# Moving the squares and RMS scales of query blocks 2 to 4 ahead of the loads in an attention + SwiGLU kernel

## The chip, the cores and the metric

The kernel runs on one core of a Trainium2 chip. The metric is device time in microseconds (us) of one execution; two executions of the kernel before were timed. The engines are named as the profile names them: PE (matrix multiply; PEld is its weight load), ACT (activations), DVE (vector), POOL (a second, general vector engine, which here also issues most loads) and SP (a queue that issues the other loads and all stores).

## The reference, cut to what matters

```python
# B=8 batches, H=8 heads, S=576 positions, D=64
scores = 0.125 * q @ k.T                       # per batch and head
scores = where(causal, -1e9, scores + minimum(-(cum_i - cum_j), 0))   # cum = cumsum(max(s, 0))
attn   = softmax(scores) @ v
x      = attn, heads side by side              # 4608 tokens x 512
rms    = sqrt(mean(x*x) + 1e-6)                # per token
xn     = x / rms * rms_g
out    = (silu(xn @ w_gate) * (xn @ w_val)) @ w_out      # 512 -> 1536 -> 512
```

## The kernel before

The work goes in turns. `attention(b)` makes one batch: 8 units (a pair of heads, `hp`, by a half of the query positions, `hf`), each with its scores on PE, `Exp` on ACT into `E` (L277), a causal mask on POOL (the affine selects, L279 and L283), the product with the values on PE (AV, L301) and a division on DVE into `x_blk` (L305, L306). `x_blk` has five blocks of 128 tokens. A block then takes three steps to reach `xnT`, the transposed and normalised input of the FFN:

- `att_square(a, tb)`: ACT squares block `tb` and sums each row (L313).
- `att_alpha(a, t0, t1)`: POOL turns the sums of several blocks into 1/rms, the tile `al` (L318, then a power, L320).
- `att_scale(a, tb)`: DVE multiplies the block by `al` (L323). `att_out(a, tb)`: four transposes on PE into `psX` (L330), then DVE writes `xnT` (L334).

Blocks 0 and 1 are complete after the fifth unit and take these steps inside `attention`. Blocks 2 to 4 are complete only after the last unit; they are this case's subject.

The FFN is cut into 9 chunks of 512 tokens. `ffn1(c)` has 12 groups: 16 matmuls of 256 columns or 8 of 512 into a pair of PSUM banks `psD` (L345, two pairs in turn), then `Silu` on ACT (L351) and a product on DVE into `H_sb` (L352). Here group n is called g0 to g11. Between groups `ffn1` runs fillers, each with a position between 0 and 1: a filler at p stands behind the first group for which (i + 1) / 12 >= p. The second half, `ffn2_steps` (L373, with the copy L378), is dealt out inside the next `attention`. So chunk c follows attention of batch c, and its first groups run before blocks 2 to 4 of that batch are in `xnT`. Everything is in program order: each engine takes its instructions in the order in which the program lists them, and waits for the one in front.

The fillers of chunk c hold, besides the three blocks: `load_kq(c + 2)` and `load_v(c + 2)` at 0.1 (five loads each of k and q on POOL, five of v on SP), `prep_v(c + 1)` on POOL (L237, five, from 0.2) with `prep_w` (L248), and the transposes of k and q of batch c + 1 (L211; for batch 1 L201, with DVE packs L191) from 0.4, or 0.66 in chunk 0. Ahead of chunk 0 stand, on POOL, the loads of k and q of batch 1 (L111), of `w_out` (L124) and of v (L118).

Of the kernel before, what the change touches and what calls it, by code (L numbers as in the profile page):

```python
# [10 lines left out]
def kernel(  # L11
# [83 lines left out]
    def ps_x():  # L95
        return pp.tile([128, CC, 128], bf16, name="psX", tag="AT", bufs=2)
# [156 lines left out]
    def att_begin(b):  # L253
        a = Att()
        a.b = b
        a.x = mp.tile([128, NB, DM], bf16, name="x_blk", tag="x_blk", bufs=2)
        a.ss = mp.tile([128, NB], fp32, name="ss", tag="ss", bufs=2)
        a.al = mp.tile([128, 2, NB], fp32, name="al", tag="al", bufs=2)
        a.E = {}
        return a  # L260

    def unit_scores(a, u):
        hp, hf = u % HP, u // HP
        st = ps_pair()
        if hf == 0:
            groups = ((0, 0, 0, 256), (1, 256, 128, 384))
        else:
            groups = ((2, 0, 256, 512), (3, 256, 384, 576), (4, 448, 512, 576))
        for i, (kb, c0, q0, q1) in enumerate(groups):
            for j in range(2):  # L270
                rs = slice(j * 64, j * 64 + 64)
                nc.tensor.matmul(  # L272
                    st[:, j, c0 : c0 + q1 - q0], lhsT=KT[rs, hp, kb * 128 : kb * 128 + 128],
                    rhs=QT[rs, hp, q0:q1],
                    start=(i == 0), stop=(i == len(groups) - 1))
        E = a.E[u] = mp.tile([128, 2, DM], bf16, name="E", tag="E", bufs=7)
        nc.scalar.activation(out=E, in_=st, func=AF.Exp, scale=0.125)  # L277
        diag = E.rearrange("p j (c n) -> p (j c) n", n=128)[:, 0:8:2, :]
        nc.gpsimd.affine_select(out=diag, in_=diag, pattern=[[0, 4], [1, 128]],  # L279
                                compare_op=ALU.is_ge, fill=0.0, base=0, channel_multiplier=-1)  # L280
        if hf == 1:
            last = E[:, :, 448:512]
            nc.gpsimd.affine_select(out=last, in_=last, pattern=[[0, 2], [1, 64]],  # L283
                                    compare_op=ALU.is_ge, fill=0.0, base=0,
                                    channel_multiplier=-1)
# [26 lines left out]
    def att_square(a, tb):  # L312
        nc.scalar.activation(out=sq_scr[:, 0:DM], in_=a.x[:, tb, :], func=AF.Square,  # L313
                             accum_out=a.ss[:, tb : tb + 1])

    def att_alpha(a, t0, t1):
        m, y = a.al[:, 0, t0:t1], a.al[:, 1, t0:t1]
        nc.gpsimd.tensor_scalar(out=m, in0=a.ss[:, t0:t1], scalar1=1.0 / DM, scalar2=1e-6,  # L318
                                op0=ALU.mult, op1=ALU.add)
        nc.gpsimd.tensor_tensor(out=y, in0=m, in1=mhalf[:, 0 : t1 - t0], op=ALU.pow)  # L320

    def att_scale(a, tb):
        nc.vector.tensor_scalar(out=a.x[:, tb, :], in0=a.x[:, tb, :],  # L323
                                scalar1=a.al[:, 1, tb : tb + 1], scalar2=None, op0=ALU.mult)

    def att_out(a, tb):
        p0 = 64 if tb == 4 else 0
        X = ps_x()
        for cc in range(CC):
            nc.tensor.matmul(X[:, cc, :], lhsT=a.x[:, tb, cc * 128 : (cc + 1) * 128],  # L330
                             rhs=ident_bf, is_transpose=True,
                             start=(cc == 0), stop=(cc == CC - 1))
        c0 = a.b * S + tb * 128
        nc.vector.tensor_tensor(  # L334
            out=xnT[:, :, c0 : c0 + 128 - p0], in0=X[:, :, p0:128],
            in1=g_sb.unsqueeze(2).to_broadcast([128, CC, 128 - p0]), op=ALU.mult)
# [46 lines left out]
    def spread(fns, lo, hi):  # L383
        n = len(fns)
        return [(lo + (hi - lo) * i / n, f) for i, f in enumerate(fns)]
# [9 lines left out]
        f.append((0.8, lambda: prep_w(b, nc.gpsimd)))  # L395
        return f

    def tail_fillers(a, lo, hi):
        fns = [lambda tb=tb: att_square(a, tb) for tb in (2, 3, 4)]
        fns += [lambda: att_alpha(a, 2, 5)]  # L400
        fns += [lambda tb=tb: (att_scale(a, tb), att_out(a, tb)) for tb in (2, 3, 4)]
        return spread(fns, lo, hi)

    def take(filler, n):
        for _ in range(n):
            next(filler, None)

    def attention(b, filler, lead, each):
        a = att_begin(b)
        take(filler, lead[0])  # L410
        unit_scores(a, 0)
        take(filler, lead[1])
        unit_scores(a, 1)
        take(filler, lead[2])
        for u in range(2 * HP):
            if u + 2 < 2 * HP:
                unit_scores(a, u + 2)
            unit_av(a, u)
            if u == HP:
                for tb in (0, 1):  # L420
                    att_square(a, tb)
                att_alpha(a, 0, 2)
            if u == HP + 2:
                for tb in (0, 1):
                    att_scale(a, tb)
                if not each:
                    for tb in (0, 1):
                        att_out(a, tb)
            if b and u < HP:
                prep_peak(b, u)  # L430
            take(filler, each)
        if each:
            for tb in (0, 1):
                att_out(a, tb)
            for _ in filler:
                pass
        return a

    whole = [(0, DM, fb) for fb in range(FB)]
# [4 lines left out]
    with tc.manual_schedule():  # L444
        nc.sync.dma_start(out=s_all, in_=s.rearrange("b h s -> (b h) s"))
        nc.sync.dma_start(out=g_sb, in_=moe_rms_g.rearrange("(cc p) -> p cc", p=128))
        load_runs(0, 0, 0, 4)
        load_runs(0, 1, 0, 4)
        make_identity(nc, ident_bf)
        load_runs(0, 0, 4, 8)  # L450
        load_runs(0, 1, 4, 8)
        make_identity(nc, ident_F)
        load_v(0, nc.gpsimd)
        for i in range(2):
            load_w(0, i * FH, (i + 1) * FH)
            load_w(1, i * FH, (i + 1) * FH)
        nc.vector.memset(ones, 1.0)
        nc.vector.memset(w_row[:, S : NB * 128], 0.0)
        nc.vector.memset(KT[:, :, S : NB * 128], 0.0)
        nc.vector.memset(vw[64:128, 4, :, :], 0.0)  # L460
        nc.vector.memset(mhalf, -0.5)
        nc.vector.memset(k_nat[64:128, :, 4, :, :], 0.0)
        nc.vector.memset(nrm, 0.0)
        nc.vector.memset(hones, 0.0)
        nc.vector.memset(hones[0:64, 0:1], 1.0)
        nc.vector.memset(hones[64:128, 1:2], 1.0)
        decay_a()
        for g in range(2):
            prep_pack(0, 4 * g, 4 * g + 4)
            prep_pack(1, 4 * g, 4 * g + 4)  # L470
            if g == 0:
                decay_b()
            for hp in (2 * g, 2 * g + 1):
                prep_transpose(0, 0, hp)
                prep_transpose(0, 1, hp)
        prep_w(0, nc.scalar)
        for sc in range(NB):
            prep_v(0, sc, nc.vector)
        a = attention(0, iter(()), (0, 0, 0), 0)
        load_runs(1, 0)  # L480
        load_runs(1, 1)
        load_w(2, 0, 6)
        load_w(2, 6, 12)
        load_v(1, nc.gpsimd)
        for c in range(NCH):
            fillers = []
            if c < B:
                fillers += tail_fillers(a, 0.0, 0.25 if c == 0 else 0.4)
            if c == 0:
                fillers += spread([lambda hp=hp: prep_peak(0, hp) for hp in range(HP)], 0.3, 0.6)  # L490
                fillers += spread([lambda i=i: prep_norm(0, i) for i in range(3)], 0.3, 0.6)
                fillers += prep_fillers(1, 0.66, 1.0)
            elif c + 1 < B:
                fillers += prep_fillers(c + 1, 0.4, 0.98)
            if c + 2 < B:
                for w in range(2):
                    fillers.append((0.1, lambda b=c + 2, w=w: load_kq(b, w)))
                fillers.append((0.1, lambda b=c + 2: load_v(b, nc.sync)))
            if c == B:
                check_decay()  # L500
                check_all()
            Ht = ffn1(c, quarters if c == 0 else halves if c < 4 else whole, fillers)
            fl = ffn2_steps(c, Ht)
            if c + 1 < B:
                a = attention(c + 1, fl, (8, 4, 6), 3)
            else:
                for _ in fl:
                    pass
# [166 lines left out]
```

## Time and profile before

| | |
|---|---|
| median of two executions | 505.26 us (503.77 and 506.76) |
| the profiled execution | 506.42 us, of which the trace's span is 504.7 |
| PE busy | 395.9 us (78% of the span) |
| DVE, ACT, POOL busy | 230.7, 215.1, 172.3 us |
| mean granted TensorE clock | 0.925 of full |

The busy time of a row counts an engine's instructions, with matmul ends modelled. Times in rows are us from the span's start. A wait is put down to what came last before the waiting instruction. PEclk is the granted TensorE clock as a share of 2.4 GHz, so 0.50 is 1.2 GHz.

### The profile page before, as it was taken

The numbers are of one execution on the slowest core, as the hardware profiler recorded it, in microseconds if no ns is written. First come the engines' busy times: TensorE is split into PE (matmuls) and PEld (weight loads), VectorE is DVE, ScalarE is ACT, GpSimd is POOL, SyncE is SP. The second block draws the span as 40 slices with busy tenths as digits, with TensorE's granted clock in tenths as the row PEclk, the third lists the DMA queues.
The fourth block names the chain that finished last, engine by engine and source line by source line (L and its number), as shares of the span: only waits on it lengthen the run. The fifth ranks groups of instructions, "written<-read, shape, count | busy, mean of one in ns | idle before, by whom it ended". The sixth has DMA issues, their size and how long they took to land.

```text
span 504.7 us, 7722 instructions
## 1 busy us (share of the span) xinstructions
PE 395.9 (78%) x3083; PEld 226.9 (45%) x3083; DVE 230.7 (46%) x461; ACT 215.1 (43%) x351; POOL 172.3 (34%) x267
## 2 busy tenths in 40 slices
PE   3740068697799779986998699959995999697995
PEld 2530047545584558455844254425442544243442
DVE  6730035565336634563355435643564356433331
ACT  2830006583257425751565156615652566120220
POOL 8651540049204930393039403940224022000000
PEclk9985559999899989998999899989998999998898
DMA  9999950019701980199019901990110011002002
GB/s 151 199 197 195 183 26 0 2 43 153 78 0 43 144 88 2 43 129 101 1 43 121 109 0 44 113 117 1 38 46 1 0 44 44 0 1 83 1 2 88
DMA packets 97803, 33.75 MB, mean 67 GB/s; under 512 B 85856, under 2 KB 92512, under 8 KB 97760
## 3 DMA queue, kind: packets, MB, share of 16 engines
q0 software_dynamic: 63840, 16.52, 34.5%
q1 hardware_dynamic: 33920, 16.67, 14.0%
q8 instruction: 26, 0.43, 0.3%
q14 instruction: 17, 0.14, 0.1%
HBM read 37.90 MB, written 9.44 MB: 94 GB/s over the span
## 4 chain that ended last, share of the span: by engine, by line
PE 57%; DMA 12%; POOL 10%; DVE 9%; ACT 8%; issue 4%; SPq 0%; ACTq 0%; POOLq 0%
PE psD L345 35%; PE psO L373 11%; DMA v_nat<-in_v_dram 8%; PE psT L211 4%; PE psX L330 3%; DMA xnT<-in_k_dram 3%; DVE H_sb L352 3%; ACT S_sb L351 3%; DVE x_blk L323 2%; POOL al L320 2%; POOL q_nat L105 2%; PE psAV L301 2%; ACT E L277 2%; POOL E L279 2%; PE psD L272 2%
## 5 line engine op out<-in xcount | busy, mean ns | idle before, releaser
L351 ACT ACTIVATE S_sb<-psD 128x512 bf16<-128x512 f32 x108 | 64.3, 595 | 240.1 <-PE psD L345 239.7
L352 DVE TENSOR_TENSOR H_sb<-S_sb,psD 128x512 bf16<-128x512 bf16 x108 | 74.2, 687 | 165.1 <-ACT S_sb L351 165.1
L345 PE MATMUL psD<-xnT,wg_sb 128*128 128x256 bf16 (+1 forms) x624 | 121.9, 335 | 0.0
L345 PE MATMUL psD<-xnT,wv_sb 128*128 128x256 bf16 (+1 forms) x624 | 118.3, 327 | 0.0
L279 POOL TENSOR_SCALAR_AFFINE_SELECT E<-E 128x512 bf16<-128x512 bf16 x64 | 41.1, 642 | 213.1 <-ACT E L277 212.9
L373 PE MATMUL psO<-wout_sb,H_sb 128*128 128x512 bf16 x432 | 107.4, 379 | 0.0
L345 PEld LDWEIGHTS <-wv_sb 128*128 128x128 bf16 x624 | 64.1, 103 | 38.0 <-issue 5.3
L330 PE MATMUL psX<-ident_bf,x_blk 128*128 128x128 bf16 x160 | 17.4, 238 | 77.6 <-DVE x_blk L323 77.5
L345 PEld LDWEIGHTS <-wg_sb 128*128 128x128 bf16 x624 | 60.1, 104 | 30.9 <-issue 2.8
L277 ACT ACTIVATE E<-psD 128x1024 bf16<-128x1024 f32 x64 | 63.6, 1023 | 8.0 <-PE psD L272 7.7
L373 PEld LDWEIGHTS <-H_sb 128*128 128x128 bf16 x432 | 36.9, 98 | 34.9 <-issue 3.0
L330 PEld LDWEIGHTS <-x_blk 128*128 128x128 bf16 x160 | 10.6, 104 | 90.6 <-DVE x_blk L323 87.6
L378 DVE COPY osb<-psO 128x512 f32<-128x512 f32 x36 | 24.8, 688 | 29.1 <-PE psO L373 29.1
L301 PE MATMUL psAV<-vw,E 128*128 128x65 bf16 x576 | 32.3, 199 | 6.2 <-POOL E L279 4.3
L237 POOL TENSOR_TENSOR vw<-v_nat,wT 128x512 bf16<-128x512 f32 (+1 forms) x35 | 35.5, 1044 | 0.0
L301 PEld LDWEIGHTS <-E 128*128 128x128 bf16 x576 | 23.6, 100 | 20.1 <-POOL E L279 10.7
L323 DVE TENSOR_SCALAR x_blk<-x_blk,al 128x512 bf16<-128x512 bf16 x40 | 18.9, 489 | 29.8 <-POOL al L320 29.3
L306 DVE TENSOR_TENSOR x_blk<-psAV,rZ 128x256 bf16<-128x256 f32 (+1 forms) x64 | 31.4, 491 | 2.2
L334 DVE TENSOR_TENSOR xnT<-psX,g_sb 128x512 bf16<-128x512 bf16 (+1 forms) x40 | 24.8, 636 | 14.3 <-PE psX L330 13.7
L105 POOL DMA_DIRECT2D k_nat<-in_k_dram x30 | 25.8, 880 | 12.2 <-DMA wout_sb<-in_moe_w_out_dram 7.7
L272 PE MATMUL psD<-QT,KT 64*128 64x256 bf16 (+2 forms) x320 | 26.7, 266 | 0.9 <-ACT E L277 0.9
L105 POOL DMA_DIRECT2D q_nat<-in_q_dram x30 | 25.4, 901 | 1.6 <-DMA v_nat<-in_v_dram 1.6
(80 smaller groups left out, 289.9 us busy)
## 6 DMA issues: line engine op xcount, KB each, us to landing
out_dram<-osb SPq DMA_DIRECT2D x36, 256.0 KB, 2.0
v_nat<-in_v_dram SPq DMA_DIRECT2D x24, 256.0 KB, 9.7
k_nat<-in_k_dram POOLq DMA_DIRECT2D x24, 128.0 KB, 4.5
q_nat<-in_q_dram POOLq DMA_DIRECT2D x24, 128.0 KB, 7.9
v_nat<-in_v_dram POOLq DMA_DIRECT2D x8, 256.0 KB, 16.0
wg_sb<-in_moe_w_gate_dram POOLq DMA_DIRECT2D x2, 768.0 KB, 14.8
wv_sb<-in_moe_w_val_dram POOLq DMA_DIRECT2D x2, 768.0 KB, 18.6
wout_sb<-in_moe_w_out_dram POOLq DMA_DIRECT2D x2, 768.0 KB, 22.7
```

Source lines behind the costliest of these rows:

```text
L105: nc.gpsimd.dma_start(out=dst[0:n, b % 2, sc, :, :], in_=src[b, :, sc * 128 : sc * 128 + n, :].rearrange("h p d -> p h d"))
L237: eng.tensor_tensor(out=vw[0:n, sc, :, 0:64], in0=v_nat[0:n, b % 2, sc, :, :], in1=wb.unsqueeze(2).to_broadcast([n, H, D]), op=ALU.mult)
L272: nc.tensor.matmul(st[:, j, c0 : c0 + q1 - q0], lhsT=KT[rs, hp, kb * 128 : kb * 128 + 128], rhs=QT[rs, hp, q0:q1], start=(i == 0), stop=(i ...
L277: nc.scalar.activation(out=E, in_=st, func=AF.Exp, scale=0.125)
L279: nc.gpsimd.affine_select(out=diag, in_=diag, pattern=[[0, 4], [1, 128]], compare_op=ALU.is_ge, fill=0.0, base=0, channel_multiplier=-1)
L301: nc.tensor.matmul(AV[:, j, qb - q0, :], lhsT=E[:, j, c0 : c0 + 128], rhs=vw[:, kb, h, :], start=(j == 0 and i == 0), stop=(j == 1 and i = ...
L306: nc.vector.tensor_tensor(out=a.x[:, q0 : q0 + nq, hp * 128 : (hp + 1) * 128].rearrange("p t (j d) -> p j t d", j=2), in0=AV[:, :, :, 0:64 ...
L330: nc.tensor.matmul(X[:, cc, :], lhsT=a.x[:, tb, cc * 128 : (cc + 1) * 128], rhs=ident_bf, is_transpose=True, start=(cc == 0), stop=(cc == ...
L345: nc.tensor.matmul(P[:, j, i * n : (i + 1) * n], lhsT=w[:, cc, fb * 128 : (fb + 1) * 128], rhs=xnT[:, cc, t0 + o : t0 + o + n], start=(i = ...
L351: nc.scalar.activation(out=sl, in_=P[:, 0, :], func=AF.Silu)
L352: nc.vector.tensor_tensor(out=Ht[:, f0 : f0 + m, o : o + n], in0=sl.rearrange("p (i n) -> p i n", i=m), in1=P[:, 1, :].rearrange("p (i n) ...
L373: nc.tensor.matmul(O, lhsT=Ht[:, fb, tb * 128 : (tb + 1) * 128], rhs=wout_sb[:, fb, :], start=(fb == 0), stop=(fb == FB - 1))
```

## The change

The squares of blocks 2 to 4 and their `att_alpha` are no longer fillers of `ffn1`: `attention` itself runs them right behind its last unit, so that in program order they stand ahead of everything the next chunk brings, its loads included. The three scales follow at the end of `attention` (behind the transposes of blocks 0 and 1 and the last six matmuls of `ffn2`, where there are any). Only `att_out` of the three blocks stays a filler, one per group: behind g0, g1 and g2 in chunk 0, behind g1, g2 and g3 in the others (before: behind g1, g2 and g2 in chunk 0, behind g2, g3 and g4 in the others).

```diff
-    def tail_fillers(a, lo, hi):
-        fns = [lambda tb=tb: att_square(a, tb) for tb in (2, 3, 4)]
-        fns += [lambda: att_alpha(a, 2, 5)]
-        fns += [lambda tb=tb: (att_scale(a, tb), att_out(a, tb)) for tb in (2, 3, 4)]
-        return spread(fns, lo, hi)
+    def tail_fillers(a, steps):
+        return [(p, lambda tb=tb: att_out(a, tb)) for p, tb in zip(steps, (2, 3, 4))]
...
             take(filler, each)
+        for tb in (2, 3, 4):
+            att_square(a, tb)
+        att_alpha(a, 2, 5)
         if each:
             for tb in (0, 1):
                 att_out(a, tb)
             for _ in filler:
                 pass
+        for tb in (2, 3, 4):
+            att_scale(a, tb)
         return a
...
-                fillers += tail_fillers(a, 0.0, 0.25 if c == 0 else 0.4)
+                fillers += tail_fillers(a, (0.08, 0.16, 0.24) if c == 0 else (0.16, 0.25, 0.33))
```

On POOL, from the last mask of attention 1 to the values of batch 2 (L318 and L320 are `att_alpha`, L105 the loads of batch 3). Before:

```order
L283 AFFINE_SELECT E<-E 128x2x64
L105 DMA k_nat<-in_k_dram 128x8x64 x4
L105 DMA k_nat<-in_k_dram 64x8x64
L105 DMA q_nat<-in_q_dram 128x8x64 x4
L105 DMA q_nat<-in_q_dram 64x8x64
L318 TENSOR_SCALAR al<-ss 128x3
L320 TENSOR_TENSOR al<-al,mhalf 128x3
L237 TENSOR_TENSOR vw<-v_nat,wT 128x8x64 x4
```

After:

```order
L283 AFFINE_SELECT E<-E 128x2x64
L318 TENSOR_SCALAR al<-ss 128x3
L320 TENSOR_TENSOR al<-al,mhalf 128x3
L105 DMA k_nat<-in_k_dram 128x8x64 x4
L105 DMA k_nat<-in_k_dram 64x8x64
L105 DMA q_nat<-in_q_dram 128x8x64 x4
L105 DMA q_nat<-in_q_dram 64x8x64
L237 TENSOR_TENSOR vw<-v_nat,wT 128x8x64 x4
```

The two instructions of `att_alpha` have changed places with the ten loads. In chunk 0 they change places in the same way with the nineteen loads that stand there (L111, L124, L118 and L105).

On DVE, from the last division of attention 1 to g5 of chunk 1. Before:

```order
L306 TENSOR_TENSOR x_blk<-psAV,rZ 128x2x3x64
L334 TENSOR_TENSOR xnT<-psX,g_sb 128x4x128 x2
L378 COPY osb<-psO 128x512
L352 TENSOR_TENSOR H_sb<-S_sb,psD 128x2x256 x3
L323 TENSOR_SCALAR x_blk<-x_blk,al 128x512
L334 TENSOR_TENSOR xnT<-psX,g_sb 128x4x128
L352 TENSOR_TENSOR H_sb<-S_sb,psD 128x2x256
L323 TENSOR_SCALAR x_blk<-x_blk,al 128x512
L334 TENSOR_TENSOR xnT<-psX,g_sb 128x4x128
L352 TENSOR_TENSOR H_sb<-S_sb,psD 128x2x256
L323 TENSOR_SCALAR x_blk<-x_blk,al 128x512
L334 TENSOR_TENSOR xnT<-psX,g_sb 128x4x64
```

After:

```order
L306 TENSOR_TENSOR x_blk<-psAV,rZ 128x2x3x64
L334 TENSOR_TENSOR xnT<-psX,g_sb 128x4x128 x2
L378 COPY osb<-psO 128x512
L323 TENSOR_SCALAR x_blk<-x_blk,al 128x512 x3
L352 TENSOR_TENSOR H_sb<-S_sb,psD 128x2x256 x2
L334 TENSOR_TENSOR xnT<-psX,g_sb 128x4x128
L352 TENSOR_TENSOR H_sb<-S_sb,psD 128x2x256
L334 TENSOR_TENSOR xnT<-psX,g_sb 128x4x128
L352 TENSOR_TENSOR H_sb<-S_sb,psD 128x2x256
L334 TENSOR_TENSOR xnT<-psX,g_sb 128x4x64
```

The three scales (L323), which stood each behind the product (L352) of the group before its transposes, now stand together ahead of the first product.

On ACT, from the last `Exp` of attention 1 to g4 of chunk 1. Before:

```order
L277 ACTIVATE E<-psD 128x1024
L351 ACT_TABLE_LOAD
L351 ACTIVATE S_sb<-psD 128x512
L313 ACTIVATE sq_scr,ss<-x_blk 128x512 x2
L351 ACTIVATE S_sb<-psD 128x512
L313 ACTIVATE sq_scr,ss<-x_blk 128x512
L351 ACTIVATE S_sb<-psD 128x512 x3
```

After:

```order
L277 ACTIVATE E<-psD 128x1024
L313 ACTIVATE sq_scr,ss<-x_blk 128x512 x3
L351 ACT_TABLE_LOAD
L351 ACTIVATE S_sb<-psD 128x512 x5
```

The squares (L313) now stand ahead of the table load for `Silu`, and that load behind them.

## Rows read from the trace of the kernel before

**Rows 1.** The page: busy us, share of the span and instructions of each engine.

```profile
PE 395.9 (78%) x3083; PEld 226.9 (45%) x3083; DVE 230.7 (46%) x461; ACT 215.1 (43%) x351; POOL 172.3 (34%) x267
```

**Rows 2.** Waits of PE: waiting instruction, releaser; us in total, times, longest.

```profile
PE psX L330 <- DVE x_blk L323: 77.5, 25, 32.4
```

**Rows 3.** Timeline of POOL around chunk 0: start, us, instruction, idle before and releaser.

```profile
25.90 0.86 POOL L111 DMA_DIRECT2D xnT<-in_k_dram  x1
...
35.22 0.89 POOL L118 DMA_DIRECT2D v_nat<-in_v_dram  x1 [3.37 <-DMA wv_sb<-in_moe_w_val_dram]
...
61.61 0.70 POOL L105 DMA_DIRECT2D q_nat<-in_q_dram  x1
62.39 0.20 POOL L318 TENSOR_SCALAR al<-ss 128x3 f32<-128x3 f32 x1
...
63.53 5.07 POOL L237 TENSOR_TENSOR vw<-v_nat,wT 128x512 bf16<-128x512 f32 x5
68.56 0.36 POOL L248 COPY vw<-wT 128x32 bf16<-128x32 bf16 x2
104.30 0.63 POOL L279 TENSOR_SCALAR_AFFINE_SELECT E<-E 128x512 bf16<-128x512 bf16 x1 [35.38 <-ACT E L277]
```

**Rows 4.** Timeline of DVE: the last division of attention 0.

```profile
28.12 0.56 DVE L306 TENSOR_TENSOR x_blk<-psAV,rZ 128x384 bf16<-128x384 f32 x1
```

**Rows 5.** Timeline of PE in chunk 0: g1 begins, block 2 transposed.

```profile
30.47 1.04 PE L345 MATMUL psD<-xnT,wg_sb 128*128 128x256 bf16 x8
...
64.78 0.61 PE L330 MATMUL psX<-ident_bf,x_blk 128*128 128x128 bf16 x4 [32.40 <-DVE x_blk L323]
```

**Rows 6.** Windows, chunk 0 from g3, from g8: us; PE, PEld, DVE, ACT, POOL busy; PEclk.

```profile
72.53:83.75 11.22, 11.22 (x82) 8.99 (x80) 5.39 (x9) 5.49 (x10) 0.00 (x0) 0.77 0.00 0
83.75:99.60 15.85, 9.73 (x114) 8.39 (x113) 8.36 (x17) 7.51 (x14) 0.00 (x0) 1.00 0.01 2
```

**Rows 7.** Windows: chunks 1 to 7, each from g0's start to g5's start.

```profile
117.46:135.42 17.96, 11.97 (x98) 9.47 (x97) 7.42 (x12) 5.84 (x13) 12.03 (x16) 0.90 1.34 139
...
423.57:438.42 14.85, 9.82 (x54) 4.34 (x53) 6.30 (x11) 4.81 (x11) 1.04 (x2) 1.00 0.05 18
sum 121.47, PE 80.97 PEld 47.93 DVE 50.35 ACT 39.89 POOL 67.57; mean PE 11.57 PEld 6.85 DVE 7.19 ACT 5.70 POOL 9.65
```

**Rows 8.** Timeline of PE in chunk 1: g1, g2, block 4's transposes, k's, g5.

```profile
119.20 1.04 PE L345 MATMUL psD<-xnT,wg_sb 128*128 128x256 bf16 x8
...
120.95 1.04 PE L345 MATMUL psD<-xnT,wg_sb 128*128 128x256 bf16 x8
...
134.74 0.40 PE L330 MATMUL psX<-ident_bf,x_blk 128*128 128x128 bf16 x4 [1.68 <-DVE x_blk L323]
134.97 0.52 PE L211 MATMUL psT<-ident_bf,k_nat 128*128 128x128 bf16 x5
135.42 0.83 PE L345 MATMUL psD<-xnT,wg_sb 128*128 128x256 bf16 x6
```

**Rows 9.** Timeline of ACT at the start of chunk 1.

```profile
113.53 1.28 ACT L351 ACT_TABLE_LOAD   x1
119.40 0.60 ACT L351 ACTIVATE S_sb<-psD 128x512 bf16<-128x512 f32 x1 [4.59 <-PE psD L345]
119.90 0.62 ACT L313 ACTIVATE sq_scr<-x_blk 128x512 bf16<-128x512 bf16 x1
...
120.64 0.63 ACT L313 ACTIVATE sq_scr<-x_blk 128x512 bf16<-128x512 bf16 x1
```

**Rows 10.** Timeline of DVE at the start of chunk 1.

```profile
114.08 0.64 DVE L323 TENSOR_SCALAR x_blk<-x_blk,al 128x512 bf16<-128x512 bf16 x2
...
115.31 0.56 DVE L306 TENSOR_TENSOR x_blk<-psAV,rZ 128x384 bf16<-128x384 f32 x1
...
120.03 0.69 DVE L352 TENSOR_TENSOR H_sb<-S_sb,psD 128x512 bf16<-128x512 bf16 x1 [1.68 <-ACT S_sb L351]
...
124.31 1.13 DVE L323 TENSOR_SCALAR x_blk<-x_blk,al 128x512 bf16<-128x512 bf16 x1
```

## The prediction

> **What bounds the kernel now.** I read the page first: PE is busy 78% of the span and no other engine over half [rows 1], so the question is what PE waits for in the rest. The waits of PE answer it with one group: 77.5 us in 25 waits of the x transposes (L330) for the scaled block (L323), one of them 32.4 us long [rows 2]. The timelines show what stands behind it, and the reader is to see two kinds.
>
> In chunk 0 the three-block `att_alpha` starts on POOL at 62.39, although its squares could be done some 30 us earlier: the loads in front of it were issued from 25.90 to 61.61 + 0.70 = 62.31 at the pace at which earlier loads landed [rows 3]. PE stands still until 64.78, for 32.40 us [rows 5].
>
> In each of chunks 1 to 7 three short waits stand between g2 and g5: one for `att_alpha`, then two for the other scales, each of which stands on DVE behind the product of the group before (1.68 us at 134.74 [rows 8]). From g0 to g5 those chunks take 121.47 us together, 17.96 in the first and 14.85 in the last [rows 7], where five groups take 1.75 us each: g1 starts at 119.20, g2 at 120.95 [rows 8]. The granted clock is part of it: 0.90 over that stretch in chunk 1 and 1.00 in chunk 7, where the stalls are shorter [rows 7].
>
> **The change part by part.** The sum is made against the profiled execution's 506.42 us, which is 1.2 above the median of the two runs.
>
> *Chunk 0, PE's side.* The last division ends at 28.12 + 0.56 = 28.68 [rows 4]. Three squares at 0.74 (119.90 to 120.64 [rows 9]) follow on ACT: 30.96 with the waits between engines. `att_alpha` takes 1.14 (62.39 to 63.53 [rows 3]), now with no load in front: 32.15. The first scale takes 0.32 (0.64 for two [rows 10]), so block 2 can be transposed from about 32.6. The transposes now stand behind g0, which ends when g1 began before, at 30.47 [rows 5]: PE still waits, but some 2.1 us and not 32.4. Then come two groups at 1.75 and three sets of transposes at 0.23 (134.74 to 134.97 [rows 8]): 32.6 + 0.2 + 1.75 + 0.2 + 1.75 + 0.2 puts g3 at 36.8, where it was at 72.53 [rows 6]. That is 35.7 us. g3 to g7 took 11.22 at a granted clock of 0.77; at full clock they are 5 x 1.75 = 8.75, another 2.5, so g8 stands at 45.6. From g8 the packs and products of DVE set the pace, the clock is 1.00 already, and 15.85 us stay [rows 6]. The data for them is there by then: batch 1's k and q have left the queue before POOL's next wait ends. PE would reach attention 1 38.2 us earlier.
>
> *Chunk 0, POOL's side.* What is late next is POOL. Its loads are issued 6 us later at first (25.90 becomes 32.2), but the queue is still full: POOL waited until 35.22 for the landing of `wv_sb` [rows 3], a load issued long before. So I let the issues catch up and end at 62.31 as before. Then `prep_v` and `prep_w` of batch 1 take 5.03 and 0.36 [rows 3] and end at 67.8. The first mask of attention 1, at 104.30 before, can't start sooner, while PE's path would have it at 104.30 - 38.2 = 66.1. The later of the two decides: 104.30 - 67.8 = **36.5 us gained**, and 1.7 of PE's gain is given up to POOL, which also covers what a low clock behind the 2.1 us wait could cost (g1 or g2 at half speed, 1.75 more).
>
> *Chunks 1 to 7, the stalls.* With every scale done before its transposes are due, a chunk from g0 to g5 needs five groups (8.75), three sets of transposes (0.7) and, but in chunk 7, k's first transposes (0.45, 134.97 to 135.42 [rows 8]): 9.9, six times, and 9.45 in chunk 7. That is 68.9 against 121.47 [rows 7]: **52.6 us gained**. The low clock goes with the stalls and is inside this difference.
>
> *Chunks 1 to 7, what is added.* The three scales stand on DVE ahead of g0's product, and g2 needs that product, because it reuses g0's PSUM pair. In chunk 1 the last division ends at 115.87 [rows 10]; squares to 118.15, then the table load's 1.28 [rows 9], which lay hidden before: `Silu` of g0 starts at 119.45 instead of 119.40. `att_alpha` ends at 119.35, three scales of 0.32 to 0.35 at 120.4, and the product, which ran from 120.03 to 120.72 [rows 10], ends at 121.1. PE is at g2 at 120.95 + 0.23 = 121.2. So the nominal cost is nothing, with 0.1 us to spare, and each us by which the scales are late is paid in full.
>
> How late they can be the trace bounds only from both sides. A pair of scales took 0.64 at 114.08, hardly disturbed; one took 1.13 at 124.31 [rows 10], where POOL's `prep_v` began just ahead of it, as it did at 63.53 [rows 3]. In chunks 1 to 5 POOL now begins to issue loads where it began `prep_v` before, and no row has a scale wholly beside that. From nothing to 3 x 0.8 = 2.4 us a chunk: I take 0.3, near the undisturbed end, since POOL spends its time there on descriptors rather than on the data. In chunk 6 no loads are left, `prep_v` follows at once, and the row at 124.31 applies: 1.5. Chunk 7 has neither. Together **3 us lost**. It can't be a gain, because nothing is removed from DVE's queue ahead of that product.
>
> The Trainium skill, SBUF — State Buffer, section "Who interferes with whom", has a rule that speaks against this place: a DVE `tensor_scalar` in a fast two-port mode and any GpSimd instruction, descriptor writing included, exclude each other for a whole instruction, whoever starts first. The 1.13 against 0.32 agrees for compute; for the issue of loads no run here shows it. By it the loss could be 2.4 us in each of six chunks, and the sum would be 431 instead of 420.
>
> *Moved past.* `att_alpha` passes ten loads on POOL in chunks 1 to 5, which are then issued from 119.4, some 5 us later (the last `Exp` had ended when the table load began at 113.53 [rows 9], and the masks behind it take about one more). Their data is first used by k's transposes of the next chunk; chunks follow each other at (423.57 - 117.46) / 6 = 51 us [rows 7], some 43 by this forecast, so over 30 us are left. SP's loads and the stores keep their place. `prep_v` ends some 4 us later than before, about 10 us ahead of the next attention. Nothing of that is on the path.
>
> Sum: 36.5 + 52.6 - 3 = 86.1; 506.42 - 86.1 = **420 us**.
>
> **The rivals.**
>
> *Scales and POOL in each other's way.* Every scale of chunks 1 to 5 is held up as at 124.31: 2.4 instead of 0.3, and 2.4 in chunk 6, some 11 us more: 431. For it speaks that POOL won the tie at 124.31; against it the pair at 114.08, which took 0.64 [rows 10].
>
> *The loads don't catch up in chunk 0.* If the queue runs dry before the first of the later loads is described, all that follows moves by 32.2 - 25.90 = 6.3, and so does the first mask of attention 1: 426. Against it: POOL waits for landings at 35.22, that is, there is a backlog.
>
> *The clock stays low.* If PE's pauses still cost a stretch at half speed in each of chunks 1 to 6, one group there takes 1.7 more: 430. Against it: chunk 7, with waits of 1.7 us each, shows 1.00 [rows 7].
>
> *It gets slower.* The mechanism would be POOL's queue as the bound: every load behind `att_alpha` is 6.3 us later in chunk 0 and 5 in each of chunks 1 to 5, 31 us together, and if the stalls of PE only cover for loads that are late anyway, nothing comes back: 537. It decides from the point at which a load lands less than 5 us before its first use. In chunks 1 to 5 that distance is over 30 us, so only chunk 0 could show it, and there it is the rival above.
>
> *The change doesn't do what it says.* The order shows `att_alpha` ahead of the loads and the scales ahead of the products; what could fail is only that the transposes wait for something else, which would leave part of the 121.47.
>
> **How the numbers follow.** The forecast gets 0.70, scales in POOL's way 0.12, late loads 0.07, low clock 0.07, slower or no change 0.01 each, and 0.02 is left for a better result, with POOL's cap lower than I make it (PE's side alone would give 418, with no loss at the scales 415). The range reaches from 414 to 430, with most of the rivals inside. A change within 2% (10 us, about what a measurement of this kernel can tell from none) or a slower kernel would need most of both waits to come back elsewhere: faster 0.97, same 0.02, slower 0.01.
>
> **What would show it.** In the changed kernel's profile the wait of L330 for L323 should fall from 77.5 to 2 or 3 us, nearly all of it in chunk 0; `att_alpha` of chunk 0 should end near 32 and its loads still near 62; the first mask of attention 1 should wait for POOL's `prep_v` and start near 68; from g0 to g5 chunks 1 to 7 should take about 10 us each at a clock of 1.00; and g2's wait for g0's product should stay under 0.5 us. Scales of a us each, a PEclk of 0.8 in those stretches, or a first mask at 74 would prove the rivals, and a new wait of PE at g2 or in the attention stages would prove me wrong.

## The result and the profile after

The changed kernel takes **419.84 us** (median of two, 418.63 and 421.04) against 505.26: 0.831 of the time before, interval 0.816 to 0.846. Run again later beside eleven runs of the kernel before it gave 0.830 (0.828 to 0.832). The forecast was 420, the range 414 to 430. The profiled execution took 421.04 us, its span is 419.3, so 85.4 us less than the span before. Ratios and their intervals, here and below, leave out executions in a slower state that the chip falls into now and then; the medians are of all executions.

The page's first section, and the waits of PE (instruction, releaser; us in total, times, longest), of the changed kernel:

```profile
PE 380.7 (91%) x3083; PEld 223.4 (53%) x3083; DVE 227.8 (54%) x461; ACT 217.7 (52%) x351; POOL 172.3 (41%) x267
...
PE psX L330 <- DVE x_blk L323: 3.9, 2, 2.1
PE psD L345 <- DVE H_sb L352: 2.0, 1, 2.0
```

PE's 77.5 us of waiting for scaled blocks [rows 2] are 3.9; one of the two waits left stands in front of blocks 0 and 1 of attention 0 and was there before. One new wait has come, of 2.0 us.

Chunk 0 on POOL (timeline):

```profile
31.06 0.20 POOL L318 TENSOR_SCALAR al<-ss 128x3 f32<-128x3 f32 x1 [5.14 <-ACT sq_scr L313]
31.34 0.86 POOL L320 TENSOR_TENSOR al<-al,mhalf 128x3 f32<-128x3 f32 x1
32.15 0.86 POOL L111 DMA_DIRECT2D xnT<-in_k_dram  x1
...
59.65 3.36 POOL L105 DMA_DIRECT2D q_nat<-in_q_dram  x4 [0.26 <-DMA v_nat<-in_v_dram]
63.02 5.03 POOL L237 TENSOR_TENSOR vw<-v_nat,wT 128x512 bf16<-128x512 f32 x5
68.00 0.36 POOL L248 COPY vw<-wT 128x32 bf16<-128x32 bf16 x2
68.60 0.64 POOL L279 TENSOR_SCALAR_AFFINE_SELECT E<-E 128x512 bf16<-128x512 bf16 x1 [0.24 <-ACT E L277]
```

`att_alpha` starts at 31.06 and not at 62.39; the loads behind it start 6.25 us later and end at 63.01 instead of 62.31, so they catch up all but 0.7 us; the first mask of attention 1 stands at 68.60 instead of 104.30 [rows 3]. On PE the same chunk reads:

```profile
32.64 0.40 PE L330 MATMUL psX<-ident_bf,x_blk 128*128 128x128 bf16 x4 [2.09 <-DVE x_blk L323]
32.88 1.67 PE L345 MATMUL psD<-xnT,wg_sb 128*128 128x256 bf16 x8
34.34 1.91 PE L345 MATMUL psD<-xnT,wv_sb 128*128 128x256 bf16 x8
```

The wait of 32.40 us [rows 5] is 2.09, and g1 behind it runs mostly at half clock (a mean PEclk of 0.54): 3.16 us to the next transposes at 36.04, where it would be 1.75.

The windows of chunks 1 to 7, each from g0's start to g5's as in [rows 7] (columns: stretch, us, busy of PE, PEld, DVE, ACT and POOL, PEclk, DMA share, GB/s):

```profile
81.78:91.80 10.02, 10.01 (x98) 8.82 (x96) 6.13 (x11) 4.64 (x8) 8.84 (x11) 1.00 1.21 152
...
298.24:310.17 11.93, 9.92 (x59) 4.94 (x57) 8.01 (x11) 4.65 (x8) 6.51 (x9) 1.00 0.06 23
343.34:352.64 9.30, 9.30 (x53) 4.59 (x52) 5.77 (x11) 4.39 (x7) 1.05 (x2) 1.00 0.07 28
sum 71.24, PE 69.09 PEld 45.85 DVE 44.44 ACT 32.26 POOL 52.27; mean PE 9.87 PEld 6.55 DVE 6.35 ACT 4.61 POOL 7.47
```

121.47 us are 71.24, at full clock and, by these rows, with PE busy for nearly all of it but in chunk 6. That chunk holds the new wait. DVE in chunk 1 and in chunk 6, and PE in chunk 6:

```profile
83.77 1.25 DVE L323 TENSOR_SCALAR x_blk<-x_blk,al 128x512 bf16<-128x512 bf16 x3 [1.10 <-POOL al L320]
...
300.23 3.21 DVE L323 TENSOR_SCALAR x_blk<-x_blk,al 128x512 bf16<-128x512 bf16 x3 [1.10 <-POOL al L320]
```

```profile
304.09 1.02 PE L345 MATMUL psD<-xnT,wg_sb 128*128 128x512 bf16 x4 [2.01 <-DVE H_sb L352]
```

Three scales beside POOL's issue of loads take 1.25 us; beside POOL's value products, which follow `att_alpha` at once in chunk 6, 3.21, and g2 waits for the product behind them.

Counted up: 104.30 - 68.60 = 35.7 in chunk 0 and 121.47 - 71.24 = 50.2 in the others make 85.9, against 85.4 for the whole span.

### The profile page after: what moved, and what is told of

It is laid out like the page before. It is cut to its first block, busy times and chain, and to the rows that moved or that the text cites. A ratio compares the mean times of both kernels' runs of the same rounds, so it can differ in the third digit from the quotient of the medians.

```text
span 419.3 us, 7722 instructions
## 1 busy us (share of the span) xinstructions
PE 380.7 (91%) x3083; PEld 223.4 (53%) x3083; DVE 227.8 (54%) x461; ACT 217.7 (52%) x351; POOL 172.3 (41%) x267
## 4 chain that ended last, share of the span: by engine, by line
PE 71%; ACT 9%; POOL 7%; DVE 5%; issue 4%; DMA 2%; ACTq 0%; POOLq 0%
PE psD L345 44%; PE psO L373 14%; PE psT L211 4%; ACT sq_scr L313 4%; PE psAV L301 4%; PE psD L272 3%; ACT E L277 2%; POOL E L279 2%; POOL al L320 2%; ACT L277 2%; DMA v_nat<-in_v_dram 2%; PE psX L330 2%; DVE x_blk L323 2%; DVE H_sb L352 1%; POOL v_nat L118 1%
## 5 line engine op out<-in xcount | busy, mean ns | idle before, releaser
L352 DVE TENSOR_TENSOR H_sb<-S_sb,psD 128x512 bf16<-128x512 bf16 x108 | 74.0, 686 | 113.9 <-ACT S_sb L351 113.9
L345 PE MATMUL psD<-xnT,wg_sb 128*128 128x256 bf16 (+1 forms) x624 | 115.1, 321 | 2.1 <-DVE H_sb L352 2.0
L345 PE MATMUL psD<-xnT,wv_sb 128*128 128x256 bf16 (+1 forms) x624 | 113.8, 318 | 0.0
L345 PEld LDWEIGHTS <-wv_sb 128*128 128x128 bf16 x624 | 62.0, 99 | 34.6 <-issue 2.2
L345 PEld LDWEIGHTS <-wg_sb 128*128 128x128 bf16 x624 | 57.4, 99 | 30.5 <-issue 4.1
L313 ACT ACTIVATE sq_scr<-x_blk 128x512 bf16<-128x512 bf16 x40 | 25.1, 628 | 22.0 <-DVE x_blk L306 21.2
L105 POOL DMA_DIRECT2D k_nat<-in_k_dram x30 | 25.8, 873 | 8.2 <-DMA wout_sb<-in_moe_w_out_dram 5.3
L105 POOL DMA_DIRECT2D q_nat<-in_q_dram x30 | 25.4, 887 | 2.7 <-DMA k_nat<-in_k_dram 2.0
L272 PEld LDWEIGHTS <-KT 64*128 64x128 bf16 x320 | 11.1, 97 | 26.3 <-issue 24.9
L220 ACT ACTIVATE QT<-psT 128x576 bf16<-128x576 bf16 x32 | 20.7, 645 | 7.4 <-PE psT L201 6.1
```

Source lines behind the costliest of these rows:

```text
L105: nc.gpsimd.dma_start(out=dst[0:n, b % 2, sc, :, :], in_=src[b, :, sc * 128 : sc * 128 + n, :].rearrange("h p d -> p h d"))
L272: nc.tensor.matmul(st[:, j, c0 : c0 + q1 - q0], lhsT=KT[rs, hp, kb * 128 : kb * 128 + 128], rhs=QT[rs, hp, q0:q1], start=(i == 0), stop=(i ...
L345: nc.tensor.matmul(P[:, j, i * n : (i + 1) * n], lhsT=w[:, cc, fb * 128 : (fb + 1) * 128], rhs=xnT[:, cc, t0 + o : t0 + o + n], start=(i = ...
L352: nc.vector.tensor_tensor(out=Ht[:, f0 : f0 + m, o : o + n], in0=sl.rearrange("p (i n) -> p i n", i=m), in1=P[:, 1, :].rearrange("p (i n) ...
```

## Experiments

All times are medians; in brackets stand the ratio to the kernel before, run beside them on the same chip (504.5, 506.1 and 505.0 us in the three series), and its interval. Each edit is against the changed kernel unless it says otherwise; `...` marks what is left out.

### The two places apart

`only_chunk0` keeps the old fillers (named `old_tail_fillers` here) for batches 1 to 7, `only_later` for batch 0. The edit shown is that of `only_chunk0`; lines without a sign are only moved in.

```diff
+        if b == 0:                                  # only_later: b > 0
             for tb in (2, 3, 4):
                 att_square(a, tb)
             att_alpha(a, 2, 5)
...
+        if b == 0:
             for tb in (2, 3, 4):
                 att_scale(a, tb)
...
-                fillers += tail_fillers(a, (0.08, 0.16, 0.24) if c == 0 else (0.16, 0.25, 0.33))
+                fillers += (tail_fillers(a, (0.08, 0.16, 0.24)) if c == 0 else old_tail_fillers(a, 0.0, 0.4))
```

> The change is made for attention 0 and chunk 0 alone; batches 1 to 7 keep squares, alpha, scales and transposes where they were. Theory (the 36 us of chunk 0 are a wait of their own, and POOL's loads catch up behind it): 505.3 less 36 is 469 to 470 us, the first mask of attention 1 near 68.6, chunks 1 to 7 from g0 to g5 again 121 us together. Rival (the loads are late and give the gain back in chunk 1, or the gain of the whole change is not a sum of its places): 475 us or more, chunk 1 longer than 18 us from g0 to g5.

> The change is made for attentions 1 to 7 alone; attention 0 and chunk 0 stay as before. Theory: chunk 0 keeps its wait of 32.4 us, the others gain 50 us: 455 us. Rival (without chunk 0's gain something else is late): another sum than 505.3 less 50; with the theory the two halves must add up to the whole, 36 + 50 = 86.

Measured: 469.44 us (0.929, 0.925 to 0.934) and 455.84 (0.902, 0.898 to 0.905). That is 35.1 and 48.7 us, 83.8 together, where the whole gains 85 to 86. The waits of PE, first of `only_chunk0`, then of `only_later`:

```profile
PE psX L330 <- DVE x_blk L323: 43.4, 23, 2.7
```

```profile
PE psX L330 <- DVE x_blk L323: 36.0, 4, 31.7
```

Each keeps the other's waits, and the two gains add up to the whole within 2 to 3 us. One sign of the rival did come: chunk 1 of `only_chunk0` took 18.80 us from g0 to g5, where it had 17.96. But its three waits are those of before (2.64, 1.68 and 1.68 us) and none is for a load; the clock over the stretch is 0.82 instead of 0.90. So chunk 0's gain isn't given back by loads that come late.

### The two causes apart

`alpha_only` moves squares and `att_alpha` as the change does, but leaves each scale a filler ahead of its transposes, at the groups of the kernel before; `scales_only` leaves squares and `att_alpha` fillers, with the three scales directly behind.

```diff
 # alpha_only: squares and att_alpha stay behind the last unit
-        return [(p, lambda tb=tb: att_out(a, tb)) for p, tb in zip(steps, (2, 3, 4))]
+        return [(p, lambda tb=tb: (att_scale(a, tb), att_out(a, tb)))
+                for p, tb in zip(steps, (2, 3, 4))]
...
-        for tb in (2, 3, 4):
-            att_scale(a, tb)
...
-                fillers += tail_fillers(a, (0.08, 0.16, 0.24) if c == 0 else (0.16, 0.25, 0.33))
+                fillers += tail_fillers(a, (0.16, 0.25, 0.25) if c == 0 else (0.25, 0.33, 0.41))
 # scales_only, against the kernel before
-        fns += [lambda: att_alpha(a, 2, 5)]
-        fns += [lambda tb=tb: (att_scale(a, tb), att_out(a, tb)) for tb in (2, 3, 4)]
+        fns += [lambda: (att_alpha(a, 2, 5), [att_scale(a, tb) for tb in (2, 3, 4)])]
+        fns += [lambda tb=tb: att_out(a, tb) for tb in (2, 3, 4)]
```

> Squares and alpha stand directly behind the last unit as in the changed kernel, but each scale stays a filler in front of its transposes, at the groups of the kernel before. Theory (two causes: alpha behind the loads, and each scale behind the product of the group before): chunk 0 gains some 34 us; chunks 1 to 7 then all look like chunk 7 did, with three waits of 1.7 us each at full clock, 15.3 us from g0 to g5, a gain of only 15 us together: 456 us. Rival (alpha behind the loads is the whole cause): 420 to 425 us.

> Squares and alpha stay fillers behind the loads as before, but the three scales stand together directly behind alpha, and the transposes stay at the groups of the kernel before. Theory: the wait for alpha stays whole (32.4 us in chunk 0, some 2.6 in chunks 1 to 6, 1.7 in chunk 7, with its stretch at half clock); the second and third waits go, 3.4 us in each of chunks 1 to 7 and 2.7 in chunk 0, a gain of 26 us: 479 us. What is then missing to the whole (86 less 15, 34 and 26) is some 11 us, the 1.7 us of each first scale behind a product, which go only when both are moved. Rival (the scales behind the products cost nothing once alpha is in time): 500 us or more.

`scales_only` took 473.94 us (0.937, 0.933 to 0.941), 31 us gained where 26 were expected; its wait for alpha is whole:

```profile
PE psX L330 <- DVE x_blk L323: 51.7, 9, 32.9
```

`alpha_only` took **495.95 us** (0.985, 0.979 to 0.991): it gains 8 to 9 us where I expected 49 and the rival 80 to 85. Neither held. In chunk 2 of its timeline, POOL, DVE and PE one after the other:

```profile
143.31 4.31 POOL L105 DMA_DIRECT2D k_nat<-in_k_dram  x5
...
151.74 5.10 POOL L237 TENSOR_TENSOR vw<-v_nat,wT 128x512 bf16<-128x512 f32 x5
```

```profile
148.07 0.55 DVE L323 TENSOR_SCALAR x_blk<-x_blk,al 128x512 bf16<-128x512 bf16 x1
...
152.09 4.91 DVE L323 TENSOR_SCALAR x_blk<-x_blk,al 128x512 bf16<-128x512 bf16 x1
...
162.60 0.34 DVE L323 TENSOR_SCALAR x_blk<-x_blk,al 128x512 bf16<-128x512 bf16 x1
```

```profile
157.05 0.61 PE L330 MATMUL psX<-ident_bf,x_blk 128*128 128x128 bf16 x4 [6.24 <-DVE x_blk L323]
```

Block 3's scale, 0.34 us alone, begins while POOL is in the first of its five products and ends as the row of products does. PE waits 6.24 us instead of 1.7, and the group behind runs at half clock. What brings the two together is the order on POOL. The same chunk before, on POOL:

```profile
165.80 4.32 POOL L105 DMA_DIRECT2D k_nat<-in_k_dram  x5
...
175.53 5.07 POOL L237 TENSOR_TENSOR vw<-v_nat,wT 128x512 bf16<-128x512 f32 x5
```

Its g0 starts at 168.74 there and at 141.39 in `alpha_only`. Counted from it, the loads come at -2.9 us before and at 1.9 now, since they stand behind `att_alpha`, and the products behind the loads at 6.8 before and at 10.4 now. Before, they met block 2's scale and were over when block 3's came; now they fall on block 3's. In chunk 0 a pair of packs meets them in the same way (4.75 us instead of 0.62):

```profile
62.49 4.75 DVE L191 COPY xnT<-xnT 96x768 bf16<-96x768 bf16 x2
```

So I formed another theory: the changed kernel gains from the scales' place also because there they are over before POOL's products begin. `alpha_act` tests it by taking the scales off DVE in `alpha_only`.

```diff
+            nc.scalar.activation(out=a.x[:, tb, :], in_=a.x[:, tb, :], func=AF.Copy,
+                                 scale=a.al[:, 1, tb : tb + 1])      # tb 2 to 4 instead of DVE
```

> The run alpha_only (squares and alpha early, each scale still a filler ahead of its transposes), with the scales of blocks 2 to 4 on ACT instead of DVE. Theory (alpha_only lost some 35 us because single scales on DVE, and in chunk 0 a pair of packs, met the run of value products on POOL and were held until it ended, 4.9 us in chunks 2 to 4): with no scale on DVE those stalls go, the three waits of PE stay at about 1.5 us each: 453 us, or 460 if chunk 0's packs still meet the products. Rival (alpha_only is slow for another reason, the place of the scales behind the products of the FFN): 485 us or more.

Measured: 454.55 us (0.897, 0.893 to 0.902). The 41 us are back, although the scales still stand behind the groups: PE waits for them 24 times for 34.1 us, at most 2.0 each, and the one long stall left is that of the packs (the waits of PE; lines of this run stand four further down, and L327 is the scale on ACT):

```profile
PE psX L334 <- ACT x_blk L327: 34.1, 24, 2.0
PE psT L201 <- DVE xnT L191: 13.6, 7, 6.4
```

Windows from g0 to g5, chunk 2 and the sum of chunks 1 to 7, first of `alpha_only`, then of `alpha_act`:

```profile
141.39:163.24 21.85, 12.05 (x99) 9.68 (x98) 11.43 (x12) 6.03 (x10) 14.92 (x19) 0.84 1.22 120
sum 136.33, PE 80.45 PEld 48.88 DVE 67.05 ACT 41.15 POOL 82.08; mean PE 11.49 PEld 6.98 DVE 9.58 ACT 5.88 POOL 11.72
```

```profile
138.51:153.37 14.86, 10.29 (x99) 8.64 (x98) 5.88 (x9) 7.86 (x13) 13.95 (x17) 1.00 1.52 162
sum 102.55, PE 71.01 PEld 44.51 DVE 40.80 ACT 53.95 POOL 76.54; mean PE 10.14 PEld 6.36 DVE 5.83 ACT 7.71 POOL 10.93
```

With alpha alone moved these seven chunks take longer than before the change (136.33 for 121.47). The profiled executions of the two runs differ by 35.4 us, and 32.0 of that lie in chunks 1 to 5, where the products meet a scale; chunks 6 and 7, where hardly one is touched, differ by 1.7. The theory is shown: what cost `alpha_only` its gain was DVE's scales beside POOL's products, with the low clock behind such stalls.

### How POOL and DVE get in each other's way

`prepv_first` puts the value products ahead of the loads in chunks 1 to 5, as they stand in chunk 6 anyway. `prepv_late_scale` adds two tiny reductions of `al` on DVE ahead of the scales; they write to a column of `al` that nothing reads any more (L439 in the rows below).

```diff
-        f += spread([lambda sc=sc: prep_v(b, sc, nc.gpsimd) for sc in range(NB)], 0.2, 0.8)
+        v0, v1 = (0.05, 0.06) if 2 <= b <= 6 else (0.2, 0.8)
+        f += spread([lambda sc=sc: prep_v(b, sc, nc.gpsimd) for sc in range(NB)], v0, v1)
...
+        for _ in range(2):                          # prepv_late_scale only
+            nc.vector.tensor_reduce(out=a.al[:, 0, 2:3], in_=a.al[:, 1, 2:5],
+                                    axis=AX.X, op=ALU.max)
```

> The changed kernel, with the five value products of the next batch on POOL ahead of the loads in chunks 1 to 5, as they stand in chunk 6, where the three scales took 3.21 us and g2 waited 2.0. Theory (DVE's scales and POOL's products on data exclude each other, POOL's issue of loads hardly touches them): the scales take 3.2 instead of 1.25 us and g2 waits 2 us in five more chunks: 10 us slower than the changed kernel, 429 to 430. Rival (chunk 6's wait comes from its groups of 512 columns or from the end of the loads): within 2 us of the changed kernel.

> The run prepv_first (value products directly behind alpha on POOL in chunks 1 to 5), with two tiny reductions of alpha ahead of the three scales on DVE in all chunks, which write to a column that nobody reads again, so that the first scale arrives some 0.3 us into POOL's first product and not 0.05. Theory (the moment of arrival decides whether a scale is held for one product, 1.1 us, or for the whole run, 4.9): the first scale takes 4 to 5 us in chunks 1 to 6, g2 waits 4 us instead of 2: some 12 us slower than prepv_first, 445. Rival (the number of things in the queue or the loads decide): scales stay at 1.1 us each and the time within 3 us of 433.

`prepv_first` took 433.48 us (0.855, 0.853 to 0.857), by the ratios 12.7 more than the changed kernel beside it (`after_again`, below), where 10 were expected. Its waits of PE, and windows of chunks 1 and 2:

```profile
PE psD L345 <- DVE H_sb L352: 12.0, 6, 2.0
```

```profile
80.27:93.92 13.65, 11.68 (x98) 9.72 (x97) 8.01 (x11) 4.64 (x8) 12.74 (x15) 0.87 1.18 149
127.27:139.26 11.99, 10.02 (x98) 8.83 (x97) 8.01 (x11) 4.64 (x8) 11.08 (x13) 1.00 1.03 149
```

Six waits of 2.0 us in place of one: chunk 6's wait is the neighbourhood of the products, not its wider groups. The profiled executions differ by 15.0 us: 10 are the waits, and in chunks 1, 3 and 5 a stretch at half clock follows (0.87 over the whole), as in the first of these rows, 1.7 us each.

`prepv_late_scale` took 432.99 us (0.854, 0.848 to 0.859): no slower, so its theory falls. In chunk 1, POOL and then DVE:

```profile
83.02 5.17 POOL L237 TENSOR_TENSOR vw<-v_nat,wT 128x512 bf16<-128x512 f32 x5
```

```profile
83.08 0.35 DVE L439 TENSOR_REDUCE al<-al 128x1 f32<-128x3 f32 x2 [1.10 <-POOL al L320]
83.35 2.95 DVE L323 TENSOR_SCALAR x_blk<-x_blk,al 128x512 bf16<-128x512 bf16 x3
```

The first scale comes 0.33 us into the row of products, as in `alpha_only` (0.35), and still all three are through in 2.95. A later arrival is not what makes one scale wait for the whole row. `alpha_only` itself says the same: in its chunk 1 block 3's scale also came 0.35 us in (100.19 for 99.84) and took 1.94, not 4.91.

### The place of the transposes, and of the scales among themselves

`outs_late` puts the transposes back at the groups of the kernel before, one group later (in chunk 0 the third keeps its place); `split_scales` leaves only block 2's scale ahead of g0's product in chunks 1 to 7; `split_late0` is that with chunk 0's transposes as in `outs_late`. `after_again` is the changed kernel and `split_again` is `split_scales` once more, each as the measure for the runs beside it.

```diff
 # outs_late
-                fillers += tail_fillers(a, (0.08, 0.16, 0.24) if c == 0 else (0.16, 0.25, 0.33))
+                fillers += tail_fillers(a, (0.16, 0.25, 0.25) if c == 0 else (0.25, 0.33, 0.41))
 # split_scales
+        f = [(0.05, lambda: att_scale(a, 3)), (0.12, lambda: att_scale(a, 4))] if a.b else []
+        return f + [(p, lambda tb=tb: att_out(a, tb)) for p, tb in zip(steps, (2, 3, 4))]
...
-        for tb in (2, 3, 4):
+        for tb in (2,) if b else (2, 3, 4):
             att_scale(a, tb)
 # split_late0: split_scales, and
+                fillers += tail_fillers(a, (0.16, 0.25, 0.25) if c == 0 else (0.16, 0.25, 0.33))
```

> The changed kernel once more, as the measure for the three beside it: 418 to 421 us.

> The changed kernel, with the transposes of blocks 2 to 4 at the groups of the kernel before (one group later). Theory (the place of the transposes is not what was gained, only the place of alpha and scales; and in chunk 0 POOL caps what PE can gain): chunk 0 loses its 2.1 us wait and the low clock behind it, but the first mask of attention 1 still starts at 68.4 since POOL is busy until then; the other chunks stay at 10 us: 418.5 to 420, within 1 us of the changed kernel. Rival (POOL is no cap, PE's path alone decides): 3 us or more faster.

> The changed kernel, with only block 2's scale ahead of g0's product in chunks 1 to 7; block 3's stands behind g0's product and block 4's behind g1's. Theory (g2 waits for g0's product, which stands behind all three scales): chunk 6 loses its 2.0 us wait, the other chunks a tenth or two each: 2 to 3 us faster than the changed kernel, 417 us. Rival (the wait only moves to the transposes of blocks 3 and 4): no faster.

Measured: 419.70, **423.09** and **414.25** us (0.830, 0.828 to 0.832; 0.836, 0.834 to 0.838; 0.820, 0.817 to 0.822). `outs_late` was expected within 1 us and is 3.4 slower. In chunk 0 the wait of 2.09 us did go, but two others of 0.58 and 1.56 us (g2's for g0's product, g3's for `xnT`) came in its place; no half clock followed them, and the first mask stood at 67.27 for 68.29 in `after_again`. POOL had been done 1.13 us before it in both, so POOL was no cap there, against my expectation. In the other chunks block 2's transposes had covered part of g2's wait: windows of `outs_late`, chunk 1 and chunk 6, and its waits of PE:

```profile
80.46:90.72 10.26, 10.02 (x98) 8.82 (x97) 5.80 (x10) 4.88 (x8) 9.35 (x12) 1.00 1.24 154
298.10:311.95 13.85, 11.61 (x59) 5.49 (x58) 7.67 (x10) 4.88 (x8) 6.51 (x9) 0.88 0.06 20
```

```profile
PE psD L345 <- DVE H_sb L352: 4.1, 7, 2.2
```

Chunk 1 is 0.24 longer than in the changed kernel, chunk 6 1.92, with a stretch at half clock; chunks 1 to 7 together take 74.42 for 71.24. So the earlier place of the transposes is worth some 3 us of its own there, against my expectation. `split_scales` was expected at 417 and took 414.25, 5.4 less than the changed kernel; from g0 to g5 chunks 1 to 7 give the expected 3.0 of it (68.20 for 71.24), chunk 6 most of all (9.84 for 11.93):

```profile
81.22:91.08 9.86, 9.86 (x99) 8.80 (x97) 6.54 (x11) 4.64 (x8) 8.95 (x12) 1.00 1.17 151
296.79:306.63 9.84, 9.84 (x58) 4.91 (x56) 6.72 (x11) 4.64 (x8) 6.54 (x9) 1.00 0.08 28
```

> The run split_scales once more, as the measure for the one beside it: 413 to 417 us.

> The run split_scales, with the transposes of chunk 0 one group later (behind g1, g2 and g2). Theory (in chunk 0 POOL's value products and PE's path end within a microsecond of each other, so that shortening PE's path alone gains little): PE's wait of 2.1 us in chunk 0 goes, the first mask of attention 1 comes at most 1 us earlier, the time is within 1 us of split_scales. Rival (PE's path alone decides): 2 us or more faster.

Measured: 416.88 us (0.825, 0.821 to 0.829) and 414.18 (0.820, 0.817 to 0.824). The intervals overlap, so the two are not told apart; the first run of `split_scales` had 414.25. The first mask of attention 1 stands at 67.51 in the profile of `split_late0` and at 67.88 in that of `split_again`, which is the small gain expected. By the ratios `split_scales` beats the changed kernel by 1.2% in its first run and 0.6% in the second, and `split_late0` by 1.1%; the interval of that second run touches the changed kernel's, those of the other two are clear of it.

## Why the prediction was right, step by step

- **Chunk 0, PE's side**: block 2's transposes at "about 32.6", 2.1 us of waiting: 32.64 and 2.09. The half-speed group behind them came, as the text allowed. g3 stood at 38.48 and not at 36.8, nearly all by that group. From g8 on "15.85 us stay" was 16.69: two of the four pairs of packs on DVE ran beside POOL's issue of loads and took 1.03 us instead of 0.62. That the data of batch 1 was "there by then" was closer than the text made it: its q had not landed when POOL's next wait ended at 44.92, only by the end of the one after it, 0.9 us ahead of the first packs (POOL, then DVE):

```profile
47.78 0.89 POOL L105 DMA_DIRECT2D k_nat<-in_k_dram  x1 [2.17 <-DMA xnT<-in_q_dram]
```

```profile
48.65 0.62 DVE L191 COPY xnT<-xnT 96x768 bf16<-96x768 bf16 x2
```

- **Chunk 0, POOL's side**: the loads caught up (63.01 for 62.31). The cap of 67.8 was 68.36. But the mask did not wait for POOL, as the text said it would: it came 0.24 us after POOL was done in the profiled execution and 1.13 after in `after_again`, released by ACT each time, so PE's path decided. Across the runs the two end within about a microsecond of each other, in either order: in `only_chunk0` the mask follows POOL's copy at once. The gain of 35.7 us for 36.5 is in part luck: PE's path lost 2.4 us by itself, 1.6 to the half clock, which the text allowed for, and 0.8 to the packs, which it put at nothing, and that is close to the 1.7 that the text gave up to POOL.
- **Chunks 1 to 7**: 52.6 less 3 was 50.2. The scales beside the issue of loads cost the 0.3 us a chunk or less: the waits list none of g2 in chunks 1 to 5, and in chunk 1 g2 starts 0.40 us behind block 2's transposes (85.27 and 85.67) where g3 starts 0.23 behind block 3's (87.41 and 87.64). Chunk 6 lost 2.0 for 1.5, and that wait of g2 is the sign that the text had named for being wrong; it came in the one chunk where the text had priced it.
- **The rivals**: "scales and POOL in each other's way" needed about 3.4 us for three scales in chunks 1 to 5, where chunk 1 shows 1.25; chunk 6, with 3.21, paid about its price. Late loads cost 0.7 of 6.3. The clock is 1.00 in all seven stretches.
- **What the reasoning did not see**: it names alpha's wait and the scales' waits side by side, and the expectation of `alpha_only` then priced them one by one. `alpha_only` shows that the scales can't be left where they were: with alpha alone moved, some 41 of 50 us are lost again to POOL's products. The forecast was spared that because the change moves both, which is luck as far as the text goes. The worst price it gave a scale, 0.8 us late, is too small where the row of products holds it whole.

The Trainium skill, SBUF — State Buffer, section "Who interferes with whom", says that a DVE `tensor_scalar` in a two-port mode and a GpSimd instruction exclude each other for the whole instruction. The scales of chunk 6 and of `prepv_first`, one product each, agree; the 4.91 us of `alpha_only` is longer than any one of POOL's instructions there and goes beyond it. No run here shows which mode the scales ran in. Beside the issue of loads the scales of chunk 1 show 1.25 for 1.05, little of such a block.

## What to carry to other kernels

When a wait on the path ends at a small instruction that stands in an in-order queue behind long ones, move the small one ahead and ask at once what the long ones will then meet: here the loads were issued some 5 us later and nothing waited for them, but the products behind them moved too, and only because the scales had moved did the two miss each other. Count a short DVE copy or scale beside a row of POOL products at up to the length of that row (here 4.9 us for 0.34), not at its own. And price a step by the stage it stands in: a third-of-a-microsecond scale behind a group's product cost PE 1.7 us.

## What the runs showed of the hardware that was not expected

- A DVE scale of 0.34 us took 4.91 (4.4 to 4.9 in chunks 2 to 5 of `alpha_only`) while POOL ran five products of about 1 us back to back, and a pair of packs 5.68 in `alpha_act`; in `prepv_first` and the kernel before, a scale beside the same row of products took 1.12 to 1.13, in chunk 1 of `alpha_only` 1.94. What decides between one product, two and the whole row stays open: the moment of arrival alone doesn't (0.35 us in for 1.94 and for 4.91; 0.33 in for three scales in 2.95 in `prepv_late_scale`).
- A wait of PE of 2.1 us in chunk 0 was followed by a stretch at half clock in the changed kernel, and waits of 2.0 in chunks 1, 3 and 5 of `prepv_first` too (0.87 from g0 to g5); the same waits in its chunks 2 and 4 were not (1.00).
- The last chunk, which no edit touches, took 11.59 us from g0 to g5 in the profile of the changed kernel (PEclk 0.74), 10.31 in that of `after_again` (0.84) and 8.64 in that of `only_chunk0` (1.00). Differences of a few us between two profiled executions can be that alone.
